# Five batches for the head sums of the values, a fourth tile for the DMA transpose, and the first tile's projection in one piece

## The chip, the cores and the metric

The kernel runs on one core of a Trainium2 chip. The metric is the time of one execution in device microseconds (us). A run of the kernel takes three such times and the median is quoted. A profile is one further execution, recorded by the hardware; all stretches below are counted from the start of its span, the time from its first to its last instruction.

The core has five engines with a queue each: TensorE (PE in the profile, its weight loads PEld), VectorE (DVE), ScalarE (ACT), GpSimd (POOL) and SyncE (SP), which here issues nearly all DMAs. An engine takes its instructions strictly in the order of the program; it stops at one that waits for a semaphore, and all that stands behind it waits too.

## The reference, cut to what matters

```
x: 2048 rows of 640;  xn = layernorm(x)
q, k, v = xn @ wqkv                       # 32 heads of 20, from 640 columns each
logits[s, w] = q[s] . k[s - 2w] / sqrt(20)    w = 0..7, masked where s - 2w < 0
attn = softmax over w
o[s] = sum over w of attn[s, w] * v[s - 2w]
out = x + o @ wo + ((xn @ w_gate) * (xn @ w_up)) @ w_down     # 1536 inner columns
```

All inputs and the output are bf16.

## The kernel before, in words

**Tiles and stages.** The 2048 rows are 16 tiles of 128 rows, or 4 blocks j of 512. The 640 columns of a projection are 5 chunks (NCH). Each tile runs through `front(t)`: two halves of statistics (L540), their aggregate (L543), a root on ACT (L546), a reciprocal (L551) and the normalising step (L561, L564 or L567), which gives the rows XNS in bf16. These are then transposed to XNT, columns on partitions, in one of two ways. Tiles t < N_PE_T = 5 are transposed on TensorE: five 128x128 blocks (L595) into PSUM, and a copy from there to XNT (L605 and L607 in two parts for tile 0, in two PSUM banks; L614 in one piece for tiles 1 to 4). The other eleven tiles are transposed by a DMA from SP (L627).

**Projections.** `proj_qk` and `proj_group` multiply XNT by wqkv (L650, 128, 256 or 512 columns wide). For tiles 0 to 3, Q and K of chunks 0 to 3 go tile by tile, 20 matmuls of 128 columns each. Chunk 4 goes for a pair of tiles at once: five matmuls of 256 columns for Q and five for K. Tile 0 is special (`spread`): its 20 matmuls are in two steps, first the 12 that need the first three of the five row chunks of the weight, then the 8 that need the last two, since the weights come in two pieces. The weights of Q are loaded as WQKV pieces 0 to 2 and 3 to 4, then those of K likewise. ACT copies each result from PSUM (L655).

**Attention.** DVE multiplies Q by eight shifted views of K (L802, L847); TensorE sums the products over each head's dimensions (L913); softmax runs on ACT and DVE. For the values, v is written to DRAM and read back in shifted views VX. There are 20 units u, five for each block j. A unit is: DVE multiplies VX by the weights (L1061) into one of three slots PV, GpSimd adds pairs (L1066, two halves of a unit) into a slot SV, and TensorE sums the four partition groups of SV into one PSUM bank (`sums`, L1108): four matmuls with a 32-column weight, one for each quarter of the PSUM partitions, which run side by side in the array. ACT then copies the bank to OT (L1117). SV has NS = 5 slots, slot u % 5 for unit u, and a unit waits until the sum of unit u - 5 has been issued. Sums come in batches: units 0 and 1, and then three at a time, seven batches in all.

**Gate and up.** `gu(j)` computes 12 groups of gate (WG) and up (WU), five matmuls of 512 columns each (L1159). ACT copies the gate half from PSUM (L655). The product with the up half is made on DVE (L1168), or by way of an ACT copy of the up half to a buffer UX on GpSimd (L1185). HT is the buffer of the products of blocks 0 and 1.

**Down.** `dn(j)` multiplies by w_down and wo and adds both in PSUM (L1241): 12 matmuls for the gate products and 5 for OT, 320 columns wide (160 at the very end). DVE adds x (L1254), and SP stores.

**Order.** The order of each engine's queue is fixed when the program is built. A list scheduler (`Sched.run`) holds an estimated duration for each operation (`occ`), a priority for each task (lower goes first) and an estimated landing time for the first loads (`land`); it picks the earliest task within a small patience. Semaphore waits follow from which addresses are read and written. So a change in one place can move instructions of every engine.

Of the kernel before, what the change touches and what calls it, by code (L numbers as in the profile page):

```python
# [11 lines left out]
NCH = 5  # L12
# [9 lines left out]
TS = 128  # L22
JB = 512
# [325 lines left out]
def build_kernel(nc, A_x, A_wqkv, A_wo, B_x, B_w_gate, B_w_up, B_w_down, out):  # L349
# [39 lines left out]
    NS = 5  # L389
    SV = [sb(f"SV{i}", [128, 4, JB], at=a_pr + i * 4096) for i in range(3)]  # L390
    SV += [sb("SV3", [128, 4, JB], at=a_qk + 33024), sb("SV4", [128, 4, JB], at=a_qk + 33024 + 4096)]
    a_sc = place[0]
    place[0] += 8192
    M1 = sb("M1", [128, 2, 4, TS], at=a_sc + 4096)
# [137 lines left out]
    def front(t):  # L532
# [22 lines left out]
                   r=[("mv", t), ("rstd", t)], w=[("nmr", t)], name=f"nmr{t}", occ=0.13)  # L555

        def apply():
            if t == 0:
                for a, b in ((0, 384), (384, D)):
                    o, i = XNS[:, 0, a:b], x[:, a:b]  # L560
                    op("dve", (lambda o, i: lambda e: e.tensor_scalar(o, i, mv[:, 0:1], rstd, op0=ALU.subtract, op1=ALU.mult))(o, i),  # L561
                       r=[i, ("mv", t), ("rstd", t)], w=[o], name=f"lnap{t}", occ=0.09 + (b - a) * 0.55e-3)
            elif t < N_DVE_A:
                op("dve", lambda e: e.tensor_scalar(xs, x, mv[:, 0:1], rstd, op0=ALU.subtract, op1=ALU.mult),  # L564
                   r=[x, ("mv", t), ("rstd", t)], w=[xs], name=f"lnap{t}", occ=0.45)
            else:
                op("act", lambda e: e.activation(xs, x, ACT.Identity, bias=nmr, scale=rstd),  # L567
                   r=[x, ("nmr", t), ("rstd", t)], w=[xs], name=f"lnap{t}", occ=0.75)
            mark("apply", t)
# [4 lines left out]
        for i in range(2):  # L574
            if t == 2 and i == 0:
                yield have("apply", 1)
            if t in (1, 2) and i == 1:
                yield have("xnt", t - 1)
            yield Task("dve", lambda: stats(i), r=[x], prio=p)
        yield Task("dve", aggr, r=[("st", t, 1)], prio=p)  # L580
# [6 lines left out]
        if t < N_PE_T:  # L587
            hold = []

            def trans(*bs):  # L590
                tpvs = [PS[:, b, :].bitcast(BF16)[:, 0:NCH * 128].rearrange("p (c f) -> p c f", c=NCH) for b in bs]
                b, tpv = bs[0], tpvs[0]
                for c in range(NCH):
                    i, q = xs[:, c * 128:(c + 1) * 128], tpvs[c // 3 if len(bs) > 1 else 0][:, c, :]
                    op("pe", (lambda q, i: lambda e: e.transpose(q, i, IDENT[:]))(q, i), r=[i, IDENT[:]], w=[q],  # L595
                       name=f"tr{t}_{c}", occ=0.057, lat=0.2)
                hold.extend(zip(bs, tpvs))
                if t == 0:
                    warm(3)

            def part(lo, hi, eng):
                b, tpv = hold[lo // 3]
                a, i = o[:, lo:hi], tpv[:, lo:hi]
                if eng == "dve":
                    X = op("dve", lambda e: e.tensor_copy(a, i), r=[PS[:, b, :]], w=[a], name=f"xntcp{t}_0", occ=0.1 + 0.08 * (hi - lo))  # L605
                else:
                    X = op("act", lambda e: e.activation(a, i, ACT.Copy), r=[PS[:, b, :]], w=[a], name=f"xntcp{t}_1",  # L607
                           occ=0.12 + 0.12 * (hi - lo))
                K.free_bank(b, X)

            def copy():
                b, tpv = hold[0]
                if t < N_DVE_C:
                    X = op("dve", lambda e: e.tensor_copy(o, tpv), r=[tpv], w=[o], name=f"xntcp{t}", occ=0.49)  # L614
                else:
                    X = op("act", lambda e: e.activation(o, tpv, ACT.Copy), r=[tpv], w=[o], name=f"xntcp{t}", occ=0.75)
                K.free_bank(b, X)

            yield Task("pe", trans, r=[xs], prio=p, banks=2 if t < N_SPLIT else 1)
            if t < N_SPLIT:  # L620
                yield Task("act", lambda: part(3, NCH, "act"), r=[PS[:, hold[1][0], :]], prio=p - 1)
                yield Task("dve", lambda: part(0, 3, "dve"), r=[PS[:, hold[0][0], :]], prio=p - 1)
            else:
                yield Task("dve" if t < N_DVE_C else "act", copy, r=[PS[:, hold[0][0], :]], prio=p)
        else:
            def dmat():
                op("sp", lambda e: e.dma_start_transpose(o, xs), r=[xs], w=[o], dma=True, name=f"dtr{t}", nbytes=200e3, occ=1.25, extra=1.3)  # L627

            yield Task("sp", dmat, r=[xs], prio=1)
# [38 lines left out]
    def proj_group(items, s0, n, prio, keys):  # L668
        hold = []

        def spread(*bs):
            if bs:
                hold.append((bs[0], [(qk_dst(items[0][0], 0, 4, s0, n), PS[:, bs[0]:bs[0] + 4, 0:n], 4 * n)]))
            b, which = hold[0][0], items[0][0]
            mms([(PS[:, b + k, 0:n], which, k, s0, n) for k in range(4)], b, f"p{which}_0", range(0, 3) if bs else range(3, NCH))

        def go(b):
            parts, outs, col = [], [], 0
            for which, m0, nm in items:
                for k in range(nm):  # L680
                    parts.append((PS[:, b, col + k * n:col + (k + 1) * n], which, m0 + k, s0, n))
                outs.append((qk_dst(which, m0, nm, s0, n), bank_view(b, col, nm, n), nm * n))
                col += nm * n
            mms(parts, b, f"p{items[0][0]}_{s0}")
            hold.append((b, outs))
# [12 lines left out]
        w0 = wcols(items[0][0], 2 if wide else NCH - 1, 0)  # L698
        yield Task("pe", spread if wide else go, r=[w0, XNT[:, NCH - 1, s0 + n - TS:s0 + n]], prio=prio, banks=4 if wide else 1, contig=wide)
        if wide:  # L700
            yield Task("pe", spread, r=[wcols(items[0][0], NCH - 1, 0)], prio=prio)
        yield Task("act", ev, r=[o for _, o, _ in hold[0][1]], prio=5)

    def proj_qk():
        for pair in (0, 2):
            for which in (0, 1):
                for t in (pair, pair + 1):
                    yield have("xnt", t)
                    K.spawn(proj_group([(which, 0, 4)], t * TS, TS, FIRST + 0.5 * which if t == 0 else 10, None))
            for which in (0, 1):  # L710
                K.spawn(proj_group([(which, 4, 1)], pair * TS, 2 * TS, 10.2, None))
        for t in (4, 6):
            yield have("xnt", t + 1)
            for items in ([(0, 0, 2)], [(1, 0, 2)], [(0, 2, 2)], [(1, 2, 2)], [(0, 4, 1), (1, 4, 1)]):
# [278 lines left out]
        yield Task("sp", move, r=[L[:]], prio=4)  # L993

    NU = NJ * NCH

    def vx_loads():
        yield num(NJ, "lg")
# [16 lines left out]

    at_bank = []
    pend = []
    used = [-3, -2, -1]

    def weighted():  # L1020
# [9 lines left out]
    def unit(u):  # L1030
# [1 line left out]
        if c == 0:  # L1032
            yield have("atx", j // 2)
        yield have("vx", u)
        if u >= NS:
            yield have("sum", u - NS)
        slots = []
        for x in range(2):
            k = min(range(2 if ("sm", 1) not in done else 3), key=lambda i: used[i])
# [21 lines left out]
            op("dve", lambda e: e.tensor_tensor(p, vw, a, ALU.mult), r=[vv] + rk, w=[p], name=f"pv{u}_{x}_{r0}",  # L1061
               occ=0.09 + 1.1 * nr)

        def add(x):
            o, p = SV[u % NS][:, 2 * x:2 * x + 2, :], slots[x]
            X = op("pool", lambda e: e.tensor_tensor(o, p[:, :, 0, :], p[:, :, 1, :], ALU.add), r=[p[:]] + tokens(), w=[o],  # L1066
                   name=f"pva{u}_{x}", occ=2.36, lock=True)
            if x == 1:
# [3 lines left out]
            return Task("dve", lambda: mul(x, r0, nr), r=[v] + [PS[:, at_bank[r], :] for r in range(r0, r0 + nr)],  # L1072
                        w=[slots[x][:, :, r0:r0 + nr, :]], prio=40)

        def adder(x, slots=slots, u=u, add=add):
            yield calm
            yield Task("pool", lambda: add(x), r=[slots[x][:]], w=[SV[u % NS][:, 2 * x:2 * x + 2, :]], prio=10, lock=True)

        if c in (0, NCH - 1):
            for r in range(2):  # L1080
# [10 lines left out]
                K.spawn(adder(x))  # L1091
        mark("mul", u)
        pend.append(u)
        if len(pend) == 3 or u == 1:
            K.spawn(sums(tuple(pend)))
            pend.clear()

    def sums(us):
# [4 lines left out]
        def go(*bs):  # L1103
            hold.extend(bs)
            for u, b in zip(us, bs):
                for dq in range(4):
                    o, p = PS[32 * dq:32 * dq + 32, b, :], SV[u % NS][:, dq, :]
                    op("pe", (lambda o, p, dq: lambda e: e.matmul(o, SEL[:], p, start=True, stop=True,  # L1108
                                                                 tile_position=(0, 32 * dq)))(o, p, dq),
                       r=[SEL[:], p], w=[o], name=f"I{u}_{dq}", occ=0.054, lat=0.4, mode=1)  # L1110
                mark("sum", u)

        def ev():
            for u, b in zip(us, hold):
# [4 lines left out]
                K.free_bank(b, X)  # L1119
                bump("ot", j)  # L1120

        yield Task("pe", go, r=[SV[u % NS][:] for u in us], prio=9.7, banks=len(us), slack=0.7)
        yield Task("act", ev, r=[PS[:, b, :] for b in hold], prio=3)

    ucount = [0]
# [148 lines left out]
        yield Task("pe", down, prio=41, banks=1, keep=0 if count.get(("ot", j), 0) >= NCH else DN_KEEP, r=[WD[:], WO[:]])  # L1274
        K.spawn(tail())

    N_PE_T = 5
    N_DVE_A = 6
    N_DVE_C = 5
    N_SPLIT = 1  # L1280
    FIRST = 9
    GU_KEEP = 3
    HP_MAX = 2
# [8 lines left out]
    tch = A_wqkv.rearrange("(c k p) n -> k c p n", k=16, c=NCH)[:, :, 0, 0:32]  # L1292
    stores.append(dma(TCH[0:16], tch, w=[TCH[0:16]], name="touch", eng="act"))
    wqkv_load(0, 0, 3, land=5.3)
    x_load(1, land=5.5)
    wqkv_load(0, 3, NCH, land=7.2)
    wqkv_load(1, 0, 3, land=8.5)
    x_load(2, land=9.0)
    wqkv_load(1, 3, NCH, land=10.0)
# [71 lines left out]
```

## Time and profile before

| | us |
|---|---|
| median of three runs (lowest, highest) | 269.6 (269.5, 269.78) |
| the profiled execution | 269.85 |
| its span | 268.1 |

The profiled execution is 0.25 us above the median; 1.75 us of it lie around the span. The granted TensorE clock was 1.000 over the whole span.

| engine | busy us | share of the span |
|---|---|---|
| TensorE | 263.9 | 98% |
| VectorE | 223.1 | 83% |
| ScalarE | 105.4 | 39% |
| GpSimd | 130.4 | 49% |

A row of the timeline gives the start, the duration of a merged run of instructions, the engine, the line, and the tiles. Matmuls overlap in the array: a group of five with 512 columns is shown as 1.24 us long, and the next one starts 1.08 us after it. Where cost is counted below, it is from start to start.

### The profile page before, as it was taken

How to read it: one execution, taken by the hardware profiler on the slowest of the kernel's cores; microseconds unless marked ns; L12 is line 12 of the kernel's file. 1: busy time of each engine (PE TensorE's matmuls, PEld its weight loads, DVE VectorE, ACT ScalarE, POOL GpSimd, SP SyncE). 2: the span in 40 equal slices, each digit the busy share in tenths (PEclk: the TensorE clock that was granted, in tenths of full speed). 3: DMA queues.
4: the chain of work that ended last, by engine and by line, in shares of the span. 5: the costliest groups of instructions: out<-in, count | busy, mean ns of one | idle time of the engine just before them, and what ended most of it. 6: DMA issues, size and time to landing. Idle time of an engine off the chain costs nothing.

```text
span 268.1 us, 4483 instructions
## 1 busy us (share of the span) xinstructions
PE 263.9 (98%) x1783; PEld 152.8 (57%) x1783; DVE 223.1 (83%) x283; ACT 105.4 (39%) x188; POOL 130.4 (49%) x81
## 2 busy tenths in 40 slices
PE   7999999999999999999999999999999999999996
PEld 5897955444444444444444445765457654676775
DVE  4788899999999996379999989999999989992212
ACT  2459997556623222255245353024430342201000
POOL 1000000000006349800299999999999879985000
PEclk9999999999999999999999999999999999999999
DMA  6954569422324997095026853565534561022201
GB/s 209 371 184 99 100 92 379 194 98 86 112 44 132 221 235 177 0 313 108 5 50 146 213 138 79 143 177 135 145 79 131 151 197 39 28 73 64 85 27 49
DMA packets 40261, 35.58 MB, mean 133 GB/s; under 512 B 15408, under 2 KB 38448, under 8 KB 40240
## 3 DMA queue, kind: packets, MB, share of 16 engines
q1 hardware_dynamic: 39424, 33.15, 45.3%
q0 software_dynamic: 576, 2.10, 3.9%
q8 instruction: 14, 0.23, 0.4%
q10 hardware_dynamic: 240, 0.05, 0.1%
q14 instruction: 7, 0.06, 0.1%
HBM read 25.07 MB, written 5.26 MB: 113 GB/s over the span
## 4 chain that ended last, share of the span: by engine, by line
PE 96%; DMA 2%; DVE 1%; SPq 0%; issue 0%; ACT 0%
PE PS L1159 39%; PE PS L1241 28%; PE PS L650 24%; PE PS L913 3%; PE PS L1108 2%; DMA XST<-in_A_x_dram 2%; PE PS L595 0%; DVE STATS L540 0%; SPq L465 0%; DVE XNS L564 0%; DVE FOUT L1254 0%; ACT SD L546 0%; DVE XNT L605 0%; DVE MV L543 0%; DVE SD L551 0%
## 5 line engine op out<-in xcount | busy, mean ns | idle before, releaser
L1066 POOL TENSOR_TENSOR SV<-PV 128x1024 bf16<-128x1024 f32 x40 | 93.4, 2359 | 25.1 <-DVE LOG L966 19.2
L1061 DVE TENSOR_TENSOR PV<-VX,PS 128x1024 f32<-128x1024 bf16 (+1 forms) x56 | 91.8, 1670 | 0.3 <-POOL SV L1066 0.3
L650 PE MATMUL PS<-XNT,WQKV 128*128 128x512 bf16 (+2 forms) x480 | 67.0, 299 | 0.2 <-DVE XNT L605 0.2
L1159 PE MATMUL PS<-XNT,WG 128*128 128x512 bf16 x240 | 59.7, 379 | 0.0
L1159 PE MATMUL PS<-XNT,WU 128*128 128x512 bf16 x240 | 59.7, 379 | 0.0
L650 PEld LDWEIGHTS PS<-XNT,WQKV 128*128 128x128 bf16 x480 | 43.5, 114 | 22.8 <-ACT LOG L924 0.8
L1159 PEld LDWEIGHTS PS<-XNT,WU 128*128 128x128 bf16 x240 | 23.3, 98 | 28.7 <-ACT XNT L655 0.8
L1159 PEld LDWEIGHTS PS<-XNT,WG 128*128 128x128 bf16 x240 | 23.3, 98 | 28.5 <-issue 0.8
L802 DVE TENSOR_TENSOR PRD<-QT,KT 128x2048 bf16<-128x2048 bf16 x32 | 36.8, 1216 | 0.0
L1254 DVE TENSOR_TENSOR FOUT<-PS,XR 128x320 bf16<-128x320 f32 (+1 forms) x33 | 15.7, 479 | 22.2 <-PE PS L1241 22.0
L1241 PE MATMUL PS<-WD,HT 128*128 128x320 bf16 x192 | 28.7, 299 | 0.0
L655 ACT ACTIVATE HT<-PS 128x512 bf16<-128x512 f32 x24 | 14.3, 596 | 34.0 <-PE PS L1159 34.0
L1241 PE MATMUL PS<-WO,OT 128*128 128x320 bf16 (+1 forms) x165 | 27.0, 295 | 0.0
L873 POOL TENSOR_TENSOR PRF<-PRF,PRF 128x1024 f32<-128x1024 f32 x4 | 9.4, 2350 | 33.4 <-DVE PRF L847 33.4
L1168 DVE TENSOR_TENSOR HT<-HT,PS 128x512 bf16<-128x512 bf16 x24 | 16.4, 682 | 9.3 <-PE PS L1159 7.7
L1117 ACT ACTIVATE OT<-PS 128x512 bf16<-128x512 f32 x20 | 10.5, 599 | 34.4 <-PE PS L1108 34.4
L932 POOL MEMSET LOG<- 32x6 bf16 (+6 forms) x7 | 0.4, 95 | 47.6 <-ACT LOG L924 47.6
L1241 PEld LDWEIGHTS PS<-WD,HT 128*128 128x128 bf16 x192 | 18.8, 98 | 7.6
L1241 PEld LDWEIGHTS PS<-WO,OT 128*128 128x128 bf16 x165 | 15.8, 98 | 6.6 <-issue 0.8
L847 DVE TENSOR_TENSOR PRF<-PS,KT 128x1024 f32<-128x1024 f32 x16 | 19.0, 1217 | 0.2 <-DMA PRF<-PRF 0.2
L540 DVE BATCH_NORM_STATS2 STATS<-XST 128x6 f32<-128x320 bf16 x32 | 14.7, 469 | 2.3 <-DMA XST<-in_A_x_dram 2.3
L1241 PE MATMUL PS<-WD,XNT 128*128 128x320 bf16 (+1 forms) x108 | 14.6, 284 | 0.0
(59 smaller groups left out, 215.9 us busy)
## 6 DMA issues: line engine op xcount, KB each, us to landing
VX<-v_scratch SPq DMA_DIRECT2D x80, 130.0 KB, 2.9
XST<-in_A_x_dram SPq DMA_DIRECT2D x16, 160.0 KB, 5.8
v_scratch<-VST SPq DMA_DIRECT2D x4, 640.0 KB, 4.4
XR<-in_A_x_dram SPq DMA_DIRECT2D x16, 160.0 KB, 3.0
out_dram<-FOUT SPq DMA_DIRECT2D x15, 160.0 KB, 1.9
PRF<-PRF POOLq DMA_DIRECT2D x4, 512.0 KB, 9.4
WG<-in_B_w_gate_dram SPq DMA_DIRECT2D x1, 1920.0 KB, 8.0
WU<-in_B_w_up_dram SPq DMA_DIRECT2D x1, 1920.0 KB, 11.9
```

The costliest lines, as they stand in the source:

```text
L540: op("dve", lambda e: e.bn_stats(o, a), r=[a], w=[("st", t, i)], name=f"bn{t}_{i}", occ=0.49)
L650: op("pe", (lambda o, l, x, c, first: lambda e: e.matmul(o, l, x, start=first, stop=(c == NCH - 1)))(o, l, x, c, first), r=[l, x], w=[o], ...
L655: X = op("act", (lambda o, i: lambda e: e.activation(o, i, ACT.Copy))(o, i), r=[i], w=[o], name=name, occ=0.12 + n * 0.9e-3)
L802: op("dve", lambda e: e.tensor_tensor(s[:], qb, kv, ALU.mult), r=[q, rk], w=[s[:]], name=f"prod{j}_{r}_{c}", occ=1.15, lock=True)
L847: X = op("dve", lambda e: e.tensor_tensor(o[:], qb, kv, ALU.mult), r=[q, rk], w=[o[:]], name=f"prow{j}_{r}_{c}_{q0}", occ=1.17)
L1061: op("dve", lambda e: e.tensor_tensor(p, vw, a, ALU.mult), r=[vv] + rk, w=[p], name=f"pv{u}_{x}_{r0}", occ=0.09 + 1.1 * nr)
L1066: X = op("pool", lambda e: e.tensor_tensor(o, p[:, :, 0, :], p[:, :, 1, :], ALU.add), r=[p[:]] + tokens(), w=[o], name=f"pva{u}_{x}", occ= ...
L1117: X = op("act", (lambda o, b: lambda e: e.activation(o, PS[:, b, :], ACT.Copy))(o, b), r=[PS[:, b, :]], w=[o], name=f"oev{u}", occ=0.58)
L1159: op("pe", (lambda l, x, c: lambda e: e.matmul(PS[:, b, :], l, x, start=(c == 0), stop=(c == NCH - 1)))(l, x, c), r=[l, x], w=[PS[:, b, :] ...
L1168: X = op("dve", lambda e: e.tensor_tensor(h, h, PS[:, hold[1], :], ALU.mult), r=[h, PS[:, hold[1], :]], w=[h], name=f"h{m}_{j}", occ=0.65)
L1241: op("pe", (lambda l, x, i: lambda e: e.matmul(dst, l, x, start=(i == 0), stop=(i == n - 1)))(l, x, i), r=[l, x], w=[PS[:, b, :]], name=f" ...
L1254: X = op("dve", lambda e: e.tensor_tensor(o, PS[:, b, 0:wid], xr, ALU.add), r=[PS[:, b, :], xr], w=[o], name=f"fin{t}_{nb}", occ=0.15 + wi ...
```

## The change

- **Sums.** Batches end with units 1, 4, 9, 14 and 19 (BATCH): five batches of 2, 3, 5, 5 and 5 units. SV has three more slots, SV5 to SV7, at the address of HT, whose first half holds the gate products of block 0; they come into use once the down matmuls of block 0 have been issued. Slots are taken from a list, and a slot returns to it when its sum has been issued.
- **Tile 4** is transposed by DMA (N_PE_T = 4), so twelve tiles go that way.
- **Tiles 0 and 1** (N_SPLIT = 2) are normalised in two parts, transposed into two banks, and copied from there in two parts. For tile 0 both copies are on ACT; for tile 1 the first is on DVE and the second on ACT.
- **Chunk 4 of tile 0** is projected in the same group as chunks 0 to 3: five more matmuls of 128 columns for Q and five for K. Tile 1 has its chunk 4 alone, as five matmuls of 128 columns each.
- Two estimated landing times are changed, and tile 1 no longer waits in the DVE order for the copy of tile 0.

```diff
+    SV += [sb(f"SV{5 + i}", [128, 4, JB], at=a_ra + i * 4096) for i in range(3)]
+    sv_free = list(range(NS))
...
-            if t == 0:
+            if t < N_SPLIT:
                 for a, b in ((0, 384), (384, D)):
-                    o, i = XNS[:, 0, a:b], x[:, a:b]
+                    o, i = XNS[:, t, a:b], x[:, a:b]
...
-            if t in (1, 2) and i == 1:
+            if t == 2 and i == 1:
                 yield have("xnt", t - 1)
...
             if t < N_SPLIT:
+                e = "act" if t == 0 else "dve"
+                yield Task(e, lambda: part(0, 3, e), r=[PS[:, hold[0][0], :]], prio=p - 1)
                 yield Task("act", lambda: part(3, NCH, "act"), r=[PS[:, hold[1][0], :]], prio=p - 1)
-                yield Task("dve", lambda: part(0, 3, "dve"), r=[PS[:, hold[0][0], :]], prio=p - 1)
...
+            if not bs:
+                mms([(PS[:, b, n:2 * n], which, 4, s0, n)], b, f"p{which}_0")
...
-                    K.spawn(proj_group([(which, 0, 4)], t * TS, TS, FIRST + 0.5 * which if t == 0 else 10, None))
+                    K.spawn(proj_group([(which, 0, 5 if t == 0 else 4)], t * TS, TS, FIRST + 0.5 * which if t == 0 else 10, None))
             for which in (0, 1):
-                K.spawn(proj_group([(which, 4, 1)], pair * TS, 2 * TS, 10.2, None))
+                t = pair or 1
+                K.spawn(proj_group([(which, 4, 1)], t * TS, (pair + 2 - t) * TS, 10.2, None))
...
+    BATCH = (1, 4, 9, 14, 19)
...
-        if u >= NS:
-            yield have("sum", u - NS)
+        if not more and count.get(("dn", 0), 0) >= 8:
+            more.append(1)
+            sv_free.extend(range(NS, len(SV)))
+        yield lambda: len(sv_free) > 0
+        sv_of[u] = sv_free.pop(0)
+        sv = SV[sv_of[u]]
...
-        if len(pend) == 3 or u == 1:
+        if u in BATCH:
             K.spawn(sums(tuple(pend)))
             pend.clear()
...
-                mark("sum", u)
+                sv_free.append(sv_of[u])
...
-    N_PE_T = 5
+    N_PE_T = 4
...
-    N_SPLIT = 1
+    N_SPLIT = 2
...
-    x_load(1, land=5.5)
-    wqkv_load(0, 3, NCH, land=7.2)
+    x_load(1, land=5.7)
+    wqkv_load(0, 3, NCH, land=7.0)
```

The scheduler then sets a new order. In the built program the queues differ from before in these places. **TensorE, start:** 25 matmuls of Q of tile 0, the transposes of tile 1, 45 matmuls (12 of K of tile 0, 20 of Q of tile 1, 13 of K of tile 0), the transposes of tile 2, 40 matmuls (K of tile 1, Q of tile 2), the transposes of tile 3, 70 matmuls of 128 columns (chunk 4 of tile 1 for Q, K of tile 2, Q and K of tile 3, chunk 4 of tile 1 for K), ten of 256, four groups of V instead of three, and then the 256-column matmuls of tiles 4 and 5. **TensorE, end:** gate and up of block 3 now run to their end after the down matmuls of block 2; the last batch of sums follows at once, and then the down matmuls of block 3. Before, gate and up ended ahead of the down matmuls of block 2. **GpSimd:** 15 gate products instead of 12, the last two of them behind the last addition of values; DVE has 33 instead of 36. **SP:** the DMA transpose of tile 4 stands ahead of that of tile 5, and some stores and loads of x in the second half move ahead of loads of VX.

More of the change, by code (lines that the diff above doesn't have):

```diff
@@ L672, in spread @@
             if bs:
-                hold.append((bs[0], [(qk_dst(items[0][0], 0, 4, s0, n), PS[:, bs[0]:bs[0] + 4, 0:n], 4 * n)]))
+                hold.append((bs[0], [(qk_dst(items[0][0], 0, 4, s0, n), PS[:, bs[0]:bs[0] + 4, 0:n], 4 * n),
+                                     (qk_dst(items[0][0], 4, 1, s0, n), bank_view(bs[0], n, 1, n), n)]))
             b, which = hold[0][0], items[0][0]
             mms([(PS[:, b + k, 0:n], which, k, s0, n) for k in range(4)], b, f"p{which}_0", range(0, 3) if bs else range(3, NCH))
+            if not bs:
+                mms([(PS[:, b, n:2 * n], which, 4, s0, n)], b, f"p{which}_0")
         def go(b):
@@ L1017, in build_kernel @@
     pend = []
+    more = []
+    sv_of = {}
     used = [-3, -2, -1]
@@ L1062, in mul, with add @@
                occ=0.09 + 1.1 * nr)
-        def add(x):
-            o, p = SV[u % NS][:, 2 * x:2 * x + 2, :], slots[x]
+        def add(x, u=u, sv=sv, slots=slots):
+            o, p = sv[:, 2 * x:2 * x + 2, :], slots[x]
             X = op("pool", lambda e: e.tensor_tensor(o, p[:, :, 0, :], p[:, :, 1, :], ALU.add), r=[p[:]] + tokens(), w=[o],
@@ L1073, in mt, with adder @@
                         w=[slots[x][:, :, r0:r0 + nr, :]], prio=40)
-        def adder(x, slots=slots, u=u, add=add):
+        def adder(x, slots=slots, sv=sv, add=add):
             yield calm
-            yield Task("pool", lambda: add(x), r=[slots[x][:]], w=[SV[u % NS][:, 2 * x:2 * x + 2, :]], prio=10, lock=True)
+            yield Task("pool", lambda: add(x), r=[slots[x][:]], w=[sv[:, 2 * x:2 * x + 2, :]], prio=10, lock=True)
         if c in (0, NCH - 1):
@@ L1106, in go @@
                 for dq in range(4):
-                    o, p = PS[32 * dq:32 * dq + 32, b, :], SV[u % NS][:, dq, :]
+                    o, p = PS[32 * dq:32 * dq + 32, b, :], SV[sv_of[u]][:, dq, :]
                     op("pe", (lambda o, p, dq: lambda e: e.matmul(o, SEL[:], p, start=True, stop=True,
@@ L1120, in ev @@
                 bump("ot", j)
-        yield Task("pe", go, r=[SV[u % NS][:] for u in us], prio=9.7, banks=len(us), slack=0.7)
+        yield Task("pe", go, r=[SV[sv_of[u]][:] for u in us], prio=9.7, banks=len(us), slack=0.7)
         yield Task("act", ev, r=[PS[:, b, :] for b in hold], prio=3)
```

## The prediction

> **What bounds the kernel now.** I read the busy times first, then the chain of waits that ended last, then the waits of TensorE alone, then its timeline at the start and around the head sums.
>
> ```profile
> PE 263.9 (98%) x1783; PEld 152.8 (57%) x1783; DVE 223.1 (83%) x283; ACT 105.4 (39%) x188; POOL 130.4 (49%) x81
> ...
> PE 96%; DMA 2%; DVE 1%; SPq 0%; issue 0%; ACT 0%
> ```
>
> ```profile
> PE PS L634 <- DVE EPSC L468: 1.3, 1, 1.3
> PE PS L595 <- DVE XNS L564: 0.3, 1, 0.3
> PE PS L650 <- DVE XNT L605: 0.2, 1, 0.2
> ```
>
> TensorE is 98% busy, and 96% of the last chain is TensorE. It waits three times, all before 8.4 us. From then on its queue sets the end: what leaves the queue shortens the run, if nothing that the queue needs is later than its new, earlier turn. The start decides much:
>
> ```profile
> 8.34 0.45 PE L595 MATMUL PS<-IDENT,XNS 128*128 128x128 bf16 x5 [0.34 <-DVE XNS L564]
> 8.76 3.55 PE L650 MATMUL PS<-XNT,WQKV 128*128 128x128 bf16 x60
> 12.14 0.44 PE L595 MATMUL PS<-IDENT,XNS 128*128 128x128 bf16 x5
> 12.42 2.06 PE L650 MATMUL PS<-XNT,WQKV 128*128 128x256 bf16 x25
> 14.32 0.44 PE L595 MATMUL PS<-IDENT,XNS 128*128 128x128 bf16 x5
> 14.60 2.94 PE L650 MATMUL PS<-XNT,WQKV 128*128 128x256 bf16 x45
> 17.38 0.44 PE L595 MATMUL PS<-IDENT,XNS 128*128 128x128 bf16 x5
> 17.66 14.56 PE L650 MATMUL PS<-XNT,WQKV 128*128 128x128 bf16 x127
> ```
>
> The reader is to count from start to start. Five transposes take 0.28 us (12.14 to 12.42; the same at 14.32 and 17.38). Sixty matmuls of 128 columns take 3.38, 0.0563 each. In the first row the transposes take 0.42: 0.14 too long. The DMA view explains it: the first piece of K's weights is issued at 2.75 and lands 6.0 later, at 8.75, just when K starts. One more wait is hidden in a busy slice:
>
> ```profile
> 13.17 1.16 PEld L650 LDWEIGHTS PS<-XNT,WQKV 128*128 128x128 bf16 x20 [0.30 <-DVE XNT L614]
> ```
>
> The five 256-column matmuls before it take 0.55 of the 0.75 us from 12.42 to 13.17; the other 0.20 are a wait for the copy of tile 2 out of PSUM.
>
> **The change, part by part.**
>
> *Front, up to 8.76 us.* Tile 1's statistics lose the copy of tile 0 in front of their second half (DVE row of 0.34 us, some 0.26 in effect), so tile 1 is normalised at about 8.0 to 8.2 instead of 8.28, and its transposes end near 8.4. Q of tile 0 can begin near 6.35, when the three warm-up matmuls have left TensorE, instead of 6.69: the ACT copy of three chunks, between its rows of 0.38 us (256 columns) and 0.60 (512), starts when the third block is transposed. None of this shortens the run: the next matmuls are K of tile 0, whose weights land at 8.75. What it buys is room: five matmuls for chunk 4 of Q fit ahead of 8.76. If the transposes of tile 1 came 0.4 later than I think, they would push K back one for one.
>
> *Chunk 4 after 8.76.* Out: ten matmuls of 256 columns. The long row from 17.66 gives 0.109 each (29.31 us of the chain for 20 of 128, 110 of 256 and 75 of 512 columns, the latter at 0.2158), so 1.09 us. In: fifteen of 128, at 0.0563 0.845. Gain 0.25. [...]
>
> *The copy of tile 2.* Its transposes are now followed by 20 matmuls of K of tile 1, 1.13 us, which cover its copy (row 0.49). The 0.20 go. In exchange TensorE comes to the transposes earlier than DVE delivers, and that is what is late next. Tile 2 of x lands at 9.16 (issued 3.26, plus 5.9), against 9.24 for its statistics before: it is normalised at 11.32 instead of 11.37. TensorE is there at 8.76 + 45 x 0.0563 = 11.29; the transposes begin at about 11.38, a wait of 0.09. Tile 3: bn of half, copy of tile 2 at 11.87, second half, aggregate (0.21), root (0.29), reciprocal (0.16), normalising (0.45), with the gaps between them as before, end near 13.95. TensorE is there at 11.66 + 40 x 0.0563 = 13.91 and waits 0.09. The bounds for these waits: 0, if DVE keeps up, and 0.5 in all, if tile 3 is no earlier than at its 14.32 of before. I take 0.18.
>
> *Tile 4.* Out: five transposes on TensorE, 0.28 us, and a DVE copy of 0.49 that nothing waits for. In: one DMA transpose, first of its kind in SP's queue, ahead of tile 5's. The trace has eleven: 1.2 us of SP each and 2.6 to landing, the first 1.41 and 2.7. Tile 4 was normalised at 16.14 to 16.59, so its transpose is issued near 16.5 and lands near 19.3; tile 5's, issued at 18.93 before, still finds SP free. The tiles' first users, the 256-column matmuls, start at 23.1 before and near 23.5 now (a fourth V group is ahead of them). Slack 2 us or more. Without it the cost would be the whole wait. [...] by the row, TensorE gives up 0.28, and the DMA's latency lies beside other work. I take the row.
>
> *Head sums.* Between full-array groups, a batch costs this:
>
> ```profile
> 141.54 1.24 PE L1159 MATMUL PS<-XNT,WU 128*128 128x512 bf16 x5
> 142.72 0.61 PE L1108 MATMUL PS<-SV,SEL 128*32 128x512 bf16 x8
> 143.26 1.25 PE L1159 MATMUL PS<-XNT,WG 128*128 128x512 bf16 x5
> ...
> 160.54 1.24 PE L1159 MATMUL PS<-XNT,WG 128*128 128x512 bf16 x5
> 161.71 0.83 PE L1108 MATMUL PS<-SV,SEL 128*32 128x512 bf16 x12
> 162.48 1.25 PE L1159 MATMUL PS<-XNT,WU 128*128 128x512 bf16 x5
> ```
>
> A group of five lasts 1.08 from start to start, so the batch of two units takes 143.26 - 142.62 = 0.64 us and that of three 162.48 - 161.62 = 0.86. A unit is 0.22, and each batch carries 0.20 besides: a gap of 0.10 ahead of it and 0.10 behind. Seven batches become five: 0.40 gained. The sums wait longer for their fifth unit, and the down matmuls for five ACT copies (rows of 0.60, 3.0 in all) instead of three. In the built order 24 down matmuls (3.26 us) stand between a five-unit batch and the first use of OT, which covers the copies with about 1 us left. The SV writes by GpSimd wait for sums that are long done.
>
> *The end of GpSimd's queue.* The trace does not show this. Before, the last additions ended with 2 us to spare:
>
> ```profile
> 239.99 4.66 POOL L1066 TENSOR_TENSOR SV<-PV 128x1024 bf16<-128x1024 f32 x2 [1.23 <-DVE PV L1061]
> ```
>
> That is 244.65; the last sum is at 246.6. Now two gate products (1.16 each) stand behind the last addition, and by the built program the eleventh matmul of block 3's down stage needs the second. Both chains run from one event T, the end of the ninth up group, issued near T. GpSimd: matmul tail and ACT copy, 1.07 after T's last matmul; product 1.11, additions 2.32 and 2.32, products 1.11 and 1.16: T + 9.1. TensorE: six groups 6.7, a batch of five 1.3, ten matmuls 1.36: T + 9.3. So it fits by 0.2. Bounds: no wait, or, if GpSimd has no idle time left to take the three added products (3 x 1.12 behind 244.65, end near 248.0 against a need near 247.2), 0.8. I take 0.03, nearest to the first, because DVE kept GpSimd idle for 5.7 us in seven waits, which is room for 3.4.
>
> **Sum.** -0.25 - 0.20 - 0.28 - 0.40 + 0.18 + 0.03 = -0.92 us. Span 267.2, execution 268.95; the median of before is 0.25 below its profiled execution, so 268.7 for the median.
>
> **Rivals.**
>
> *A. Handed back in front.* DVE's chain for tile 3 stays at 14.32, or ACT's copies hold a PSUM bank at 20 to 36 us, where ACT is full. For it: TensorE now arrives within 0.1 of DVE twice. Against it: the x tile lands earlier than it is needed, and no bank wait is in the list. Then 0.35 to 0.5 is lost: gain 0.4 to 0.55, time near 269.1.
>
> *B. The last batch holds the end (slower).* Place: the wait for the last two gate products on GpSimd. Price: each us of GpSimd beyond 247.2 is a us of the run. It eats the gain of 0.95 at 248.15 and makes the kernel slower beyond the noise from 248.7 on, 4 us later than GpSimd ended before. For it: three more products, and slots and additions in lockstep with DVE. Against it: 3.4 us are added, 5.7 were idle. Time 270.3 if it came at 248.8.
>
> *C. The waits at 11.3 and 13.9 vanish*, and the last fits: -1.13, time 268.5. This lies in the main case's range.
>
> *D. The batches save nothing*, because a five-unit batch waits for its fifth unit: -0.5, time 269.1. Against it: unit 9's addition ended at 187.5 in the trace, and its sum now comes seven groups (7.6 us) behind the down matmuls of block 0, which ended at 182.9: near 190.
>
> **How the numbers follow.** Main case (with C) 0.81, A and D 0.14, B 0.05. What a measurement can tell from no change is 0.2%, 0.54 us, so the bound is 269.06. The main case is faster (0.81), of A and D a third (0.05), the rest the same (0.10); B is slower in most cases (0.04). The main case's bounds are 268.4 (no waits) and 269.0 (0.5 in front); with the scatter of the runs, 0.14 each way, and A, the range is 268.2 to 269.2.
>
> **What would show it.** Right: K of tile 0 still starts near 8.76; transposes of tile 2 and 3 near 11.4 and 14.0; batches of five take 1.30 between their neighbours; TensorE has short waits at L595 alone. Wrong: a wait of TensorE on GpSimd near 247; one on L627 near 23.5; K earlier than 8.7, which would mean that the weights did not hold it.

## The result, and the profile after

| | before | changed kernel |
|---|---|---|
| median (lowest, highest), us | 269.65 (269.49, 269.96), 6 runs | 268.85 (268.64, 268.9), 6 runs |
| ratio, 95% interval | | 0.9967 [0.9955, 0.998] |
| the profiled execution | 269.85 | 268.9 |
| its span | 268.1 | 267.4 |
| TensorE's last end | 265.74 | 264.81 |

The change makes the kernel 0.3% faster, more than the 0.2% that can be told from none. TensorE ends 0.93 us earlier; the span shrinks by 0.7 only, since the last store ended 2.6 us behind TensorE and not 2.4.

The page of the changed kernel, the busy line and the chain that ended last:

```profile
PE 263.2 (98%) x1788; PEld 153.1 (57%) x1788; DVE 220.8 (83%) x279; ACT 107.3 (40%) x195; POOL 133.5 (50%) x84
...
PE 98%; ACT 0%; DVE 0%; issue 0%
```

TensorE's queue is still the bound. The waits of TensorE (two, where there were three) come next:

```profile
PE PS L637 <- DVE EPSC L470: 1.3, 1, 1.3
PE PS L653 <- ACT QT L658: 0.3, 1, 0.3
```

The first is the start of the run, as before. The second is new, and no step of the prediction has it: a matmul of the projection waits for ACT's copy of Q out of PSUM. TensorE's timeline at the start shows where (start, duration, then what ran):

```profile
6.46 1.65 PE L653 MATMUL PS<-XNT,WQKV 128*128 128x128 bf16 x25
7.95 0.44 PE L597 MATMUL PS<-IDENT,XNS 128*128 128x128 bf16 x5
8.37 0.31 PE L653 MATMUL PS<-XNT,WQKV 128*128 128x128 bf16 x2
8.97 2.60 PE L653 MATMUL PS<-XNT,WQKV 128*128 128x128 bf16 x43 [0.30 <-ACT QT L658]
11.40 0.44 PE L597 MATMUL PS<-IDENT,XNS 128*128 128x128 bf16 x5
11.68 2.40 PE L653 MATMUL PS<-XNT,WQKV 128*128 128x128 bf16 x40
14.08 0.45 PE L597 MATMUL PS<-IDENT,XNS 128*128 128x128 bf16 x5
```

K of tile 0 starts at 8.37, not at 8.76, because its weights landed at 8.32 in this execution (8.71 in the profile of before). Two matmuls later it stops until 8.97. ACT's timeline gives the reason:

```profile
8.15 0.77 ACT L658 ACTIVATE QT<-PS 128x512 bf16<-128x512 f32 x2 [1.00 <-PE PS L653]
```

Q of tile 0 now has two copies, chunks 0 to 3 and chunk 4, which end at 8.92. Chunk 4 lies in the first of Q's four PSUM banks, and K's third matmul writes to that bank (an edit below tests this). So ACT's copy, and not the weights, decides when K gets going; in effect K starts at 8.97 - 2 x 0.056 = 8.86. The transposes of tile 2 follow without a wait. Those of tile 3 come 2.40 us after 40 matmuls that take 40 x 0.0558 = 2.23, a wait of 0.17 for DVE.

The batches of five, and the end of GpSimd's queue:

```profile
188.02 1.24 PE L1173 MATMUL PS<-XNT,WG 128*128 128x512 bf16 x5
189.19 1.26 PE L1122 MATMUL PS<-SV,SEL 128*32 128x512 bf16 x20
190.39 1.80 PE L1255 MATMUL PS<-WD,HT 128*128 128x320 bf16 x12
```

```profile
239.23 1.16 POOL L1199 TENSOR_TENSOR XNT<-XNT,UX 128x512 bf16<-128x512 bf16 x1 [1.86 <-ACT UX L658]
240.35 4.65 POOL L1080 TENSOR_TENSOR SV<-PV 128x1024 bf16<-128x1024 f32 x2
244.96 2.27 POOL L1199 TENSOR_TENSOR XNT<-XNT,UX 128x512 bf16<-128x512 bf16 x2
```

A batch of five takes 190.39 - 188.02 - 1.08 = 1.29 us. That is 0.065 for each of its 20 matmuls, where one of 512 columns over the full array takes 0.216 (1.08 for five): the four of a unit overlap. The last gate product ends at 244.96 + 2.27 = 247.23; its user is the eleventh down matmul of block 3. These start at 246.12, 0.136 us apart, so the eleventh stands at 246.12 + 10 x 0.136 = 247.48. It fits by 0.25.

### The profile page after: what moved, and what is told of

Read it like the earlier page. It is cut to its first block, busy times and chain, and to the rows that moved or that the text cites. A ratio compares the mean times of both kernels' runs of the same rounds, so it can differ in the third digit from the quotient of the medians.

```text
span 267.4 us, 4492 instructions
## 1 busy us (share of the span) xinstructions
PE 263.2 (98%) x1788; PEld 153.1 (57%) x1788; DVE 220.8 (83%) x279; ACT 107.3 (40%) x195; POOL 133.5 (50%) x84
## 4 chain that ended last, share of the span: by engine, by line
PE 98%; ACT 0%; DVE 0%; issue 0%
PE PS L1173 39%; PE PS L1255 28%; PE PS L653 25%; PE PS L920 3%; PE PS L1122 2%; PE PS L637 2%; PE PS L597 1%; ACT QT L658 0%; DVE FOUT L1268 0%; DVE ZERO L469 0%; DVE EPSC L470 0%
## 5 line engine op out<-in xcount | busy, mean ns | idle before, releaser
L658 ACT ACTIVATE UX<-PS 128x512 bf16<-128x512 f32 x15 | 9.0, 598 | 38.5 <-PE PS L1173 38.5
L658 ACT ACTIVATE XNT<-PS 128x512 bf16<-128x512 f32 x12 | 7.2, 597 | 27.5 <-PE PS L1173 27.5
```

Of the source, the lines that this page charges most:

```text
L658: X = op("act", (lambda o, i: lambda e: e.activation(o, i, ACT.Copy))(o, i), r=[i], w=[o], name=name, occ=0.12 + n * 0.9e-3)
```

## The experiments

Kernels that were measured together share their runs of the kernel before, so the median of before differs a little from one experiment to another. Each measurement has one profiled execution. Beside the medians I use TensorE's last end in it, and split it at the start of the first sum of Q times K (46.57 us in the changed kernel, 47.06 before): the first stretch holds the start and tile 4, the second the batches.

### The parts alone

Batches alone (the start and tile 4 as before):

```diff
+    SV += [sb(f"SV{5 + i}", [128, 4, JB], at=a_ra + i * 4096) for i in range(3)]
...
+    BATCH = (1, 4, 9, 14, 19)
...
```

> The kernel before, with five batches of head sums and the three more slots as the only edit; start and tile 4 as before. Theory (TensorE's queue is the bound, and a batch carries 0.20 us beside its units): two batches fewer take 0.40 us off TensorE's last end, 265.76 to 265.36, and 0.15% off the time (269.25). The three TensorE waits of before stay. Rival (the batches save nothing, since a batch of five waits for its fifth unit): 265.76, with a wait of TensorE on SV in the list. Second rival (the parts of the change only pay together): anything below -0.2 or above -0.6.

269.24 us against 269.59, ratio 0.9983 [0.9976, 0.999]. The second stretch is 264.82 - 46.59 = 218.23 us, 0.45 less than the 218.68 of before: the theory holds for the batches. TensorE's last end fell by 0.92 and not by 0.40; the other 0.47 lie in the first stretch, which this edit does not touch, and the next experiment shows where.

Tile 4 alone:

```diff
-    N_PE_T = 5
+    N_PE_T = 4
```

> The kernel before, with tile 4 transposed by DMA as the only edit. Theory (five transposes leave the queue, the DMA's latency is hidden): TensorE's last end -0.28 us, 265.76 to 265.48; no wait of TensorE on a DMA near 23.1, though the DMA takes about 4.4 us from issue to landing as in the changed kernel. Rival (the work that was behind the transposes hides them, or the DMA holds the 256-column matmuls): 265.76 or later. [...]

269.22 us, ratio 0.9988 [0.9981, 0.9994]; no wait of TensorE for the DMA. TensorE's timeline of this kernel, at the start:

```profile
7.95 0.45 PE L595 MATMUL PS<-IDENT,XNS 128*128 128x128 bf16 x5 [0.34 <-DVE XNS L564]
8.23 3.62 PE L650 MATMUL PS<-XNT,WQKV 128*128 128x128 bf16 x60
```

From the end of tile 3's transposes to the first sum it takes 46.34 - 14.15 = 32.19 us, before 47.06 - 14.60 = 32.46: the five transposes are worth 0.27. But K starts at 8.23 here, with the old start, where it started at 8.76 in the profile of before. The batches alone have it at 8.28. The profile of before had shown an execution in which K was late.

The start alone (tile 4 on TensorE, seven batches, five slots):

```diff
-    SV += [sb(f"SV{5 + i}", [128, 4, JB], at=a_ra + i * 4096) for i in range(3)]
...
-    BATCH = (1, 4, 9, 14, 19)
+    BATCH = (1, 4, 7, 10, 13, 16, 19)
...
-    N_PE_T = 4
+    N_PE_T = 5
```

> The changed kernel's start alone (chunk 4 of tile 0 with the first group, copies split for tiles 0 and 1); tile 4 on TensorE, seven batches, five slots. Theory, with what the changed kernel's trace showed (K of tile 0 starts 0.10 later in effect, since its third matmul waits for ACT's copy of Q out of the same PSUM bank; waits of 0 and 0.15 at the transposes of tiles 2 and 3): about -0.25 us at TensorE's last end, 265.76 to 265.51. Rival (start handed back in full): 265.76. The third matmul of K at about 8.97, after ACT's row of 0.77, as in the changed kernel.

270.25 us, ratio 1.002 [1.0012, 1.0029]: slower, against both expectations. In its profiled execution (269.76, one of the faster ones) TensorE ends at 265.68. The timeline of its weight loads has a wait that no other kernel has, and ACT's timeline the cause:

```profile
34.99 2.10 PEld L652 LDWEIGHTS PS<-XNT,WQKV 128*128 128x128 bf16 x11 [0.37 <-DMA XNT<-XNS]
```

```profile
20.77 0.60 ACT L657 ACTIVATE VST<-PS 128x512 bf16<-128x512 f32 x1
21.26 0.91 ACT L568 ACTIVATE XNS<-XST,SD 128x640 bf16<-128x640 bf16 x1
22.07 0.58 ACT L657 ACTIVATE VST<-PS 128x512 bf16<-128x512 f32 x1
22.55 0.29 ACT L547 ACTIVATE SD<-MV,EPSC 128x1 f32<-128x1 f32 x1
22.93 0.60 ACT L657 ACTIVATE VST<-PS 128x512 bf16<-128x512 f32 x1
23.42 0.91 ACT L568 ACTIVATE XNS<-XST,SD 128x640 bf16<-128x640 bf16 x1
```

With tile 4 on TensorE, two V copies stand between these two normalising steps of ACT, so the second starts at 23.42; in the changed kernel there is one, and it starts at 22.26. From there on each tile's DMA transpose is issued 1.15 us later than in the changed kernel, and one that took 4.2 us instead of some 2.6 (30.71 to 34.95) made TensorE wait 0.28 beyond its pitch. The median is 0.5 above this profiled execution; whether the same wait is longer there was not traced, so most of the loss has no shown cause. What follows: the scheduler's answer to this part alone is another order, and in that order the start did not pay.

### Seven batches in the changed kernel

```diff
-    BATCH = (1, 4, 9, 14, 19)
+    BATCH = (1, 4, 7, 10, 13, 16, 19)
```

> The changed kernel with the old seven batches of head sums (sizes 2, 3, 3, 3, 3, 3, 3) and all eight slots. Theory: +0.40 us at TensorE's last end, 264.82 to 265.22, and 0.15% on the time. Rival (the batches save nothing): 264.82. It also tells whether the last additions on GpSimd, rather than the size of the last batch, decide the end: the last gate product on GpSimd should again end about 0.2 us ahead of its use.

269.32 us, ratio 0.9991 [0.9984, 0.9997]. The second stretch is 265.49 - 46.81 = 218.68, as before: 0.44 for two batches. (TensorE's last end is 0.68 later than in the changed kernel's trace, where 0.40 was expected; the other 0.24 lie in the first stretch, for a reason shown under the next edit.) The expectation about GpSimd's end was not tested by this: the scheduler went back to 12 gate products on GpSimd, none of them behind the last addition, which ended at 244.41. The close fit at the end belongs to the order that comes with the five batches.

### The old start in the changed kernel, and both beside each other

The old start is put back with all its parts: the splits and copies, chunk 4, the order of tile 1's statistics and the landing estimates. Two of the places:

```diff
-                    K.spawn(proj_group([(which, 0, 5 if t == 0 else 4)], t * TS, TS, FIRST + 0.5 * which if t == 0 else 10, None))
+                    K.spawn(proj_group([(which, 0, 4)], t * TS, TS, FIRST + 0.5 * which if t == 0 else 10, None))
...
-    N_SPLIT = 2
+    N_SPLIT = 1
...
```

> The changed kernel, unaltered, beside the others on this chip, so that the three that follow have their measure. 268.85 us was its median before; TensorE's last end 264.8 where the first piece of K's weights lands near 8.35, about 265.05 where it lands near 8.8.

> The changed kernel with the start of the kernel before (chunk 4 of tile 0 with tile 1 in 256 columns, tile 1 normalised and copied in one piece); tile 4 by DMA, five batches, eight slots. Theory now (the start brings nothing: the kernels with the old start had K at 8.23 and 8.28, so the weights did not hold it, and ten matmuls of 128 columns more ahead of K and ACT's longer copy push K back by what the second part saves): TensorE's last end 8.25 + 256.54 - 0.27 = 264.5, time 268.6 to 268.9, equal to the changed kernel or up to 0.3 us below. Rival (the prediction's step: the start is worth 0.25 + 0.20 - 0.18 = 0.27): 0.27 us above the changed kernel, 269.1.

The changed kernel: 268.76 (268.65 to 268.98), ratio 0.9966 [0.9954, 0.9978]. The old start: 269.16 (268.68 to 269.37), ratio 0.9977 [0.9968, 0.9986]. Neither expectation covers this: the lowest runs are equal, as the theory said, but the old start spreads upward, to medians 0.40 apart, where the rival had 0.27 (the intervals overlap). The profiled executions belong to the lower end and agree, 264.67 and 264.59 at TensorE's last end.

The traces suggest what spreads: when tile 1 of x lands. It is issued at 1.73 in each, and landed between 5.42 and 6.49. With the old start K follows it by a fixed way, unless its weights land later still:

| kernel with the old start | tile 1 lands | K's weights land | K starts | from tile 1 |
|---|---|---|---|---|
| before | 5.85 | 8.71 | 8.76 | 2.91 |
| batches alone | 5.42 | 8.24 | 8.28 | 2.86 |
| tile 4 alone | 5.46 | 8.15 | 8.23 | 2.77 |
| old start in the changed kernel | 5.47 | 8.10 | 8.24 | 2.77 |
| the same with chunk 4 early (below) | 6.07 | 8.55 | 8.84 | 2.77 |

In the profile of before the weights held K by 0.14, with the batches alone by 0.09; in the others tile 1 alone did. With the new start and tile 1 early, neither decides, but ACT's second copy of Q, behind which K's third matmul starts:

| kernel with the new start | tile 1 lands | Q's second copy ends | K's third matmul | first sum of Q times K |
|---|---|---|---|---|
| changed kernel | 5.67 | 8.92 | 8.97 | 46.57 |
| the same again | 5.51 | 8.78 | 8.83 | 46.43 |
| seven batches | 5.44 | 9.16 | 9.21 | 46.81 |

The way from that matmul to the first sum is 37.60 us in all three. The old start with tile 4 by DMA has its first sum at 46.35, with tile 1 at 5.47. So a second theory: the new start is worth nothing where tile 1 lands early, and much where it lands late.

### Tile 1 of x made late

Two kernels, with the new and with the old start, in which two loads change places (shown for the new start):

```diff
-    x_load(1, land=5.7)
     wqkv_load(0, 3, NCH, land=7.0)
+    x_load(1, land=5.7)
```

> The changed kernel with the load of tile 1 of x issued after the second piece of Q's weights, one place (some 0.5 us) later; no engine's order is touched but the order of these two loads. Theory (the new start pays where tile 1 of x lands late: it shortens the way from that landing to K of tile 0 from 2.88 us, 5.88 to 8.76 before, to 2.5, 6.51 to 9.02 in the last kernel, and has five matmuls more behind it): with a landing at 6.0 to 6.4, K starts at 8.5 to 8.9 and TensorE ends about 258.4 after the landing, 264.5 to 264.8; time 268.7 to 269.0, much as the changed kernel. Rival (the start's worth is the same wherever tile 1 lands): the distance to the next kernel is the 0.40 us between the medians of the changed kernel and of the one with the old start.

> The kernel with the old start, tile 4 by DMA and five batches, and the same swap of two loads. Theory: K starts 2.9 us after tile 1 lands, TensorE ends about 259.2 after it, so 0.8 us above the last kernel at the same landing: 265.2 to 265.6 at landings of 6.0 to 6.4, time 269.4 to 269.8. Rival: 0.40 above the last kernel, or nothing.

New start: 269.05 (268.93 to 269.18), ratio 0.9975 [0.9965, 0.9985]. Old start: 269.64 (269.45 to 270.81), ratio 1.0005 [0.9994, 1.0015]. No run of one lies within the range of the other. The timeline of the new start, and then that of the old one:

```profile
6.59 0.89 DVE L542 BATCH_NORM_STATS2 STATS<-XST 128x6 f32<-128x320 bf16 x2 [0.94 <-DMA XST<-in_A_x_dram]
...
8.72 0.54 PE L597 MATMUL PS<-IDENT,XNS 128*128 128x128 bf16 x5 [0.76 <-DVE XNS L563]
9.10 0.67 PE L653 MATMUL PS<-XNT,WQKV 128*128 128x128 bf16 x9
```

```profile
6.51 0.49 DVE L542 BATCH_NORM_STATS2 STATS<-XST 128x6 f32<-128x320 bf16 x1 [1.10 <-DMA XST<-in_A_x_dram]
6.92 0.34 DVE L607 COPY XNT<-PS 128x384 bf16<-128x384 bf16 x1
7.18 0.48 DVE L542 BATCH_NORM_STATS2 STATS<-XST 128x6 f32<-128x320 bf16 x1
...
8.97 0.45 PE L597 MATMUL PS<-IDENT,XNS 128*128 128x128 bf16 x5 [0.34 <-DVE XNS L566]
9.26 0.55 PE L652 MATMUL PS<-XNT,WQKV 128*128 128x128 bf16 x7
```

Old: the copy of tile 0 stands between the halves of tile 1's statistics, and K comes 2.75 us after DVE gets the tile. New: 2.51. From K to the first sum the new start needs 46.78 - 9.10 = 37.68 us, the old one 47.37 - 9.26 = 38.11. Together 0.67 at the same landing, where 0.8 was expected (the 2.88 taken from before held 0.14 of weights), and 0.59 between the medians. The medians alone would not decide, since 0.59 lies half way between this 0.8 and the rival's 0.40. By the traces, one of each kernel, the second theory holds: from a landing at 5.47 to one at 6.49 the old start ends 1.02 us later (264.59, 265.61), one for one; from 5.51 to 6.57 the new start ends 0.35 later (264.67, 265.02). That the runs without a trace spread for the same reason is likely but not shown.

### Chunk 4 of both tiles ahead of Q of tile 2

In the kernel with the old start:

```diff
-                K.spawn(proj_group([(which, 4, 1)], pair * TS, 2 * TS, 10.2, None))
+                K.spawn(proj_group([(which, 4, 1)], pair * TS, 2 * TS, 10.2 if pair else 10, None))
```

> As the last, and both groups of chunk 4 of tiles 0 and 1 (ten matmuls of 256 columns, 1.09 us) stand between the transposes of tile 2 and Q of tile 2, where there were five. Theory: they cover the copy of tile 2 (0.75 us from the transposes' end), the 0.20 us that Q of tile 2 waited vanish: 0.20 below the last kernel, TensorE's last end 264.3. Rival: tile 3's transposes then wait for DVE by as much, 264.5.

271.12 us (270.66 to 273.13), ratio 1.0069 [1.0044, 1.0095]. The wait at the copy of tile 2 is gone: the 30 matmuls behind tile 2's transposes take 2.21 us without a gap. But the scheduler moved the end as well. GpSimd and TensorE, on the timeline of this kernel:

```profile
242.64 4.66 POOL L1075 TENSOR_TENSOR SV<-PV 128x1024 bf16<-128x1024 f32 x2
...
244.97 1.52 PE L1250 MATMUL PS<-WD,XNT 128*128 128x320 bf16 x10
247.25 1.16 POOL L1194 TENSOR_TENSOR XNT<-XNT,UX 128x512 bf16<-128x512 bf16 x1
248.46 0.45 PE L1250 MATMUL PS<-WD,XNT 128*128 128x320 bf16 x2 [1.97 <-POOL XNT L1194]
```

The last gate product stands behind two additions that start 2.3 us later than in the changed kernel, and twelve down matmuls now stand ahead of the last batch. The eleventh waits 2.13 us, start to start beyond its pitch. The sum, from the kernel with the old start, closes: 264.59 + 0.60 (tile 1 landed later) - 0.20 + 2.13 = 267.12; TensorE ended at 267.10: what stood behind the waiting matmul in the queue came 2.13 later with it. So the -0.20 came as expected, and the end lost ten times as much. This is the prediction's rival B, met in a neighbour of the changed kernel: place and mechanism as it said.

### The bank of chunk 4, and the statistics of tile 3

```diff
-                                     (qk_dst(items[0][0], 4, 1, s0, n), bank_view(bs[0], n, 1, n), n)]))
+                                     (qk_dst(items[0][0], 4, 1, s0, n), bank_view(bs[0] + 3, n, 1, n), n)]))
...
-                mms([(PS[:, b, n:2 * n], which, 4, s0, n)], b, f"p{which}_0")
+                mms([(PS[:, b + 3, n:2 * n], which, 4, s0, n)], b, f"p{which}_0")
```

> The changed kernel with chunk 4 of tile 0 in the last of its group's four PSUM banks, not the first. Theory (K's third matmul waits for ACT's second copy only since chunk 4 lies in the bank it needs first): it waits for the first copy alone, 0.60 instead of 0.77 us, and starts about 0.17 earlier; where the weights land near 8.35, TensorE's last end 264.65; where they land near 8.8, less is gained. Rival (the weights or DVE hold the start): no change.

268.61 (268.56 to 269.02), ratio 0.9962 [0.995, 0.9974], 0.15 below the changed kernel measured beside it; the intervals overlap widely, so no gain is shown. In its profiled execution tile 1 landed at 6.49 and held K, so the bank's own wait does not show there. It shows in the next kernel, which adds one exchange on DVE and nothing on any other queue:

```diff
-            op("dve", lambda e: e.bn_stats(o, a), r=[a], w=[("st", t, i)], name=f"bn{t}_{i}", occ=0.49)
+            op("dve", lambda e: e.bn_stats(o, a), r=[a], w=[("st", t, i)], name=f"bn{t}_{i}", occ=0.49); mark("st", t, i)
...
+                yield (lambda: t != 2 or ("st", 3, 1) in done)
                 yield Task("dve" if t < N_DVE_C else "act", copy, r=[PS[:, hold[0][0], :]], prio=p)
```

> The changed kernel with chunk 4 in the last bank, and on DVE the second half of tile 3's statistics ahead of the copy of tile 2, not behind it. Theory: DVE stood idle for 0.2 to 0.5 us there while the transposes of tile 2 ran, so tile 3 is normalised about 0.4 us earlier; the 0.165 us that TensorE waited ahead of tile 3's transposes go, and the copy of tile 2 still ends before its use at 12.8. TensorE's last end 0.16 below the kernel with the last bank alone; time 268.45, some 0.3 below the changed kernel. Rival: Q of tile 2 then waits for the later copy by as much: 268.6.

268.37 (268.22 to 268.57), ratio 0.9949 [0.9937, 0.9961]: the fastest of all, as expected (268.45), and 0.39 below the changed kernel's median, which was measured at another time on the same chip. Its timeline:

```profile
10.79 0.88 DVE L542 BATCH_NORM_STATS2 STATS<-XST 128x6 f32<-128x320 bf16 x2
11.10 0.44 PE L597 MATMUL PS<-IDENT,XNS 128*128 128x128 bf16 x5
11.38 2.40 PE L653 MATMUL PS<-XNT,WQKV 128*128 128x128 bf16 x40
11.58 0.49 DVE L616 COPY XNT<-PS 128x640 bf16<-128x640 bf16 x1
...
13.61 0.44 PE L597 MATMUL PS<-IDENT,XNS 128*128 128x128 bf16 x5
```

Both halves of the statistics run while TensorE comes to tile 2, the copy follows, and from 11.38 to 13.61 there are 2.23 us for 40 matmuls: the wait of 0.17 is gone and none took its place. K's third matmul starts at 8.66, behind the first copy of Q (8.01 + 0.60) and ahead of the end of the second (8.78): a wait of 0.19, where it was 0.46.

### Matmuls of 256 columns in halves

```diff
-                    parts.append((PS[:, b, col + k * n:col + (k + 1) * n], which, m0 + k, s0, n))
+                    for h in range(0, n, TS if n == 2 * TS else n):
+                        g = min(n, TS) if n == 2 * TS else n
+                        parts.append((PS[:, b, col + k * n + h:col + k * n + h + g], which, m0 + k, s0 + h, g))
```

> The changed kernel with every matmul of 256 columns over two tiles of x (110 of them) as two of 128 columns into the same PSUM bank, with the same copies. By the row of the trace (0.0563 us for 128 columns, 0.109 for 256): 220 x 0.0563 - 110 x 0.109 = +0.40 us at TensorE's last end. [...]

One run, 269.06 us, with its profile. From the end of tile 3's transposes to the first sum: 46.63 - 14.16 = 32.47 us, in the changed kernel 46.57 - 14.37 = 32.20. So 110 matmuls more cost 0.27 us, where 0.40 was expected, and one of 128 columns is (110 x 0.109 + 0.27) / 220 = 0.0557. The row was right, to 0.0006 us a matmul.

## Why the prediction was right, and where it was not

**The time** was right: 268.7 was said, 268.85 and 268.76 were measured; TensorE's last end fell by 0.93 for a sum of 0.92. Part of that agreement is luck of the two executions: the one of before had K late, and the start's part of the sum depends on that. Split at the first sum of Q times K:

| | predicted | the two traces | by the experiments |
|---|---|---|---|
| head sums | -0.40 | -0.44 | -0.45 alone, -0.44 undone |
| tile 4 | -0.28 | | -0.27 |
| start | -0.27 | -0.22 (0.49 - 0.27) | about 0 at a landing of 5.5 (0.08 late), -0.67 near 6.5 |
| end of GpSimd's queue | +0.03 | 0 | |

*Head sums*: right in mechanism and size. TensorE has no wait at a batch, so none waited for its fifth unit, and rival D falls.

*Tile 4*: right. Its DMA took 4.4 us, 16.74 to 21.11, where 2.7 was taken from the first row of before; the slack of two us and more that the prediction gave it covered that. The five transposes freed 0.27, where 0.28 was said.

*Front, up to 8.76 us*: this step failed, in the sentence "None of this shortens the run: the next matmuls are K of tile 0, whose weights land at 8.75." In that execution the weights happened to land late, and to hold K by 0.14 us. What stood just before them, the way from tile 1's landing to K, is the step that the new start shortens, by 0.24 (2.75 to 2.51 in the late pair), and where tile 1 lands late this does shorten the run. The prediction had written down a sign for it ("K earlier than 8.7, which would mean that the weights did not hold it"). The changed kernel's trace has K at 8.37, but there the sign misleads: the first two matmuls still waited for the weights, which landed at 8.32, and then ACT's copy of Q held K. That tile 2's and tile 3's transposes come at 11.40 and 14.08, about as predicted, is luck: the bank wait put K in effect at 8.86, near the 8.76 that was taken from the weights.

*Chunk 4*: the price of 0.0563 was right; the gain of 0.25 was counted on room that the late execution had. The step holds where tile 1 is late. Where it lands early, five matmuls more ahead of K and a second ACT copy of Q move K from 8.24 with the old start to 8.86 in effect and eat it. The bank wait is rival A's ("ACT's copies hold a PSUM bank"), at 8.4 us and not at the 20 to 36 us that were named; the argument against it, "no bank wait is in the list", looked at the list of before, which cannot have a wait that the change makes.

*Copy of tile 2* -0.20, right, no wait is left there. *Transposes*: 0.09 each were taken, 0 and 0.17 came; the sum of 0.18 is right.

*End of GpSimd's queue*: fits by 0.25, 0.2 was said. That GpSimd can hold the end was right too, as the kernel with chunk 4 early shows.

## What to carry to other kernels

A profile is one draw of when the first loads land: tile 1 of x, issued at 1.73 us, landed between 5.42 and 6.49 in these traces. Before a step at the start is priced by "the last to land", write out the way from each landing to the work, and see which comes second and by how much; a gain that depends on it is a gain for some executions only.

Look for the waits that the change itself can make: a group put into a bank that the next group needs first is one (0.46 us here). And where a scheduler orders everything, a part alone is not that part of the whole; the order has to be read again for each variant.

## What the runs showed of the hardware that was not expected

**TensorE's rate at the start varied from run to run.** The granted clock is given as 1.000 for the span, and yet the first matmuls of some traces are half as fast: 0.107 us apart at 128 columns, where later ones are 0.056. Two kernels with the same start, on TensorE's timeline, first that with seven batches and then that with halves:

```profile
6.35 2.01 PE L653 MATMUL PS<-XNT,WQKV 128*128 128x128 bf16 x25
```

```profile
6.30 1.59 PE L653 MATMUL PS<-XNT,WQKV 128*128 128x128 bf16 x25
```

In the first, matmuls of 128 columns come 0.107 us apart until 7.20 us and 0.056 apart from then on, and the next group starts at 8.19; in the second they come 0.056 apart from the beginning, and it starts at 7.74. Over all traces the change came between 4.2 us (tile 4 alone) and 7.2 (seven batches), a spread of 3 us, with TensorE busy from 1.27. What sets it was not shown. It costs the new start something: with seven batches Q of tile 0 began at 6.35, as in the second trace of the changed kernel (6.38, at 0.056), but its copies, K's third matmul and the first sum all came 0.38 us later. With the old start TensorE waits for DVE ahead of tile 1's transposes (0.27 to 0.34 us in the traces, until 7.90 at the earliest). By my estimate that wait could take up a slow stretch of its length, which no trace shows; the new start has five matmuls more there.

**A DMA transpose of 128 x 640 took 2.6 us in most cases (the median of the changed kernel's twelve), but some were slow.** Of those issued between 30 and 35 us, the one at 32.62 in the profile of before took 4.3 us from issue to landing, the one at 30.71 in the start alone 4.2, and in the changed kernel those at 31.14, 32.73 and 34.32 took 4.9, 4.1 and 3.2. The first of the changed kernel, tile 4's, took 4.4 us and the second 3.1; in the profile of before, where tile 5's is the first, it was 2.7 and 2.6. Why was not tested. Only in the start alone did a wait of TensorE for one show, 0.37 us of its weight loads up to 34.99.
